# Decay exponents from a bf16 product per four heads, a first block on weight differences, and a new order of the products, in a Mamba-2 scan with a maxout feed-forward

## The chip, the cores and the metric

The kernel runs on one core of a Trainium2 chip. Its engines are TensorE (PE: matrix products into PSUM; PEld is its weight load), VectorE (DVE), ScalarE (ACT), GpSimd (POOL) and SyncE (SP), which here issues the DMAs. Each engine works through its own instructions in program order and waits on semaphores for the others. The metric is the device time of one execution in microseconds (us), as the median of several runs.

## What is computed

Four batches of 768 tokens with eight heads go through a state-space scan, and the 3072 x 256 result goes through a maxout feed-forward with three 256 x 768 matrices and an output matrix:

```
log_a = np.log(np.clip(a, 1e-06, 1.0))
cum = np.cumsum(la, axis=-1)
L = np.exp(cum[:, :, :, None] - cum[:, :, None, :])
L = L * causal
CB = np.einsum('bhin,bhjn->bhij', Cc, Bc)
M = CB * L
y_intra = np.einsum('bhij,bhjd->bhid', M, xc)
y_inter = np.einsum('bhin,bhnd->bhid', Cc, state) * decay_to_i[:, :, :, None]
...
h = np.maximum(np.maximum(x @ w1, x @ w2), x @ w3)
return (h @ w_out).astype(np.float32)
```

The weights arrive as 64-bit floats, and the kernel turns them into 32-bit ones itself.

## The kernel before, in words

The sequence is cut into six blocks of 128 tokens (c = 0 to 5), each for all four batches (512 columns) and all eight heads. **Block 0** is computed in plain fp32: its scan, then the three up products for six feature groups of 128 (18 groups, n = 0 to 17, in the loop at L962, products L589 and L597; an fp32 product stands in the trace as two rows), then its output products (`first_down`, L780, products L792) which run inside block 1. **Blocks 1 to 5** use the three weight matrices as a base and two differences: max(x w1, x w2, x w3) = x w2 + max(x (w1-w2), x (w3-w2), 0). Every operand is split into a near part H, a far part L and a crossed part S (`split_steps` L612 for weights, `scan_y` L560 for the scan's output, `late` L710 for h), so that three fast products (fp32r) replace a slow one. A block has twelve units u, six feature groups f by two differences i. In each unit `early` (L704) makes the near and far products (`near_far` L687, products L692) into one of two up banks of PSUM and scales their sum (`raise_sum` L697, on ACT in even units and on DVE in odd ones); `late` (L710) adds the crossed products (L717) of the unit before and takes the maximum: ACT copies m (L722) for i = 0, DVE makes h (L726) and H (L730) for i = 1, POOL makes L (L731). `down_next` (L822, products L811) makes the output of the block before.

**Weights.** SP fetches twelve pieces of 512 KB (`fetch` L163). `decode` (L215) starts the conversion of one piece: ACT L191 and L200, DVE L192 and L195, POOL L201; `sign` (L221) ends it with DVE L206. In the loop over the 18 groups a sign and a decode stand at every second group. `behind` (L671) issues the steps that form and split the differences (POOL L637 and L626, ACT L625 and L622, DVE L628).

**Decays.** The scan needs L = exp(cum_i - cum_j) for 128 x 128 positions of each batch and head. SP writes the running sums to DRAM (L887) and reads them back spread over all partitions: `decay_load` L387 fills L (1 MB for two batches), `last_load` L394 fills E (eight DMAs a block). POOL masks L (`decay_masks` L400, L402), ACT takes the exponential head by head with the bias -cum_j (`decay_part` L406, L409: 128 columns an instruction, 32 a block). DVE multiplies the scores s (L501) with L (`scan_weight` L507, L509); `scan_old` and `scan_own` (L515, L530) make y, and the next block's products need y. The scan of block n = c + 1 is worked in among block c's units. s, y, A, trB, trC, w2T and fold share four att banks of PSUM.

The order is written out by hand: the strings FIRST, STEADY and LAST (L1036 to L1067) give the words of each unit, which `act` (L1069) turns into calls: Z is `early`, p `late`, d `down_next`, q `first_down`, x and z parts of the exponentials, m and n masks, b steps of `behind`, t, c, e, s0, s2, A, y the steps of the scan, a number so many waiting steps of `later`.

## Time and profile before

| | |
|---|---|
| median of 3 runs | 293.43 us (292.38 to 297.33) |
| profiled execution | 294.27 us, span 292.6 us, mean granted clock 0.975 |
| busy in the span | PE 257.2 us (88%), DVE 177.7 (61%), ACT 144.6 (49%), POOL 117.9 (40%) |
| chain that ended last | PE 54%, DVE 19%, DMA 6%, SP's queue 5%, ACT 5%, POOL 4% |
| DMA | 28.13 MB in 105018 packets, of which L from cums takes 10 DMAs of 1 MB and E 40 of 32 KB |

The span is the time from the first to the last instruction of one profiled execution; the profiled execution took 1.7 us more than its span. Busy shares are means over stages: an opening of block 0, five blocks of twelve units, and a short end. Which wait ends last in a stage is read from the waits and the timeline of that stage.

### The profile page before, as it was taken

How to read it: one execution, taken by the hardware profiler on the slowest of the kernel's cores; microseconds unless marked ns; L12 is line 12 of the kernel's file. 1: busy time of each engine (PE TensorE's matmuls, PEld its weight loads, DVE VectorE, ACT ScalarE, POOL GpSimd, SP SyncE). 2: the span in 40 equal slices, each digit the busy share in tenths (PEclk: the TensorE clock that was granted, in tenths of full speed). 3: DMA queues.
4: the chain of work that ended last, by engine and by line, in shares of the span. 5: the costliest groups of instructions: out<-in, count | busy, mean ns of one | idle time of the engine just before them, and what ended most of it. 6: DMA issues, size and time to landing. Idle time of an engine off the chain costs nothing.

```text
span 292.6 us, 5239 instructions
## 1 busy us (share of the span) xinstructions
PE 257.2 (88%) x2030; PEld 197.6 (68%) x2030; DVE 177.7 (61%) x283; ACT 144.6 (49%) x336; POOL 117.9 (40%) x105
## 2 busy tenths in 40 slices
PE   6899992897986899879899798999898999999994
PEld 4665340446855578758678586787686787979993
DVE  2586757699666454285673865766645838445452
ACT  2775745694598423785315475416573332222211
POOL 5173668318975525354151541534211113112321
PEclk9999999799999879979999999999999999999999
DMA  7979998986999110488500779101000002002002
GB/s 83 177 280 273 144 258 148 211 188 168 209 182 128 40 36 1 100 220 83 69 2 2 210 187 130 14 3 64 10 0 0 2 2 73 0 2 72 0 3 72
DMA packets 105018, 28.13 MB, mean 96 GB/s; under 512 B 75297, under 2 KB 101921, under 8 KB 104993
## 3 DMA queue, kind: packets, MB, share of 16 engines
q1 hardware_dynamic: 104688, 27.66, 46.6%
q8 instruction: 16, 0.26, 0.4%
q10 hardware_dynamic: 304, 0.13, 0.2%
q14 instruction: 10, 0.07, 0.1%
HBM read 24.54 MB, written 3.24 MB: 95 GB/s over the span
## 4 chain that ended last, share of the span: by engine, by line
PE 54%; DVE 19%; DMA 6%; SPq 5%; ACT 5%; POOL 4%; issue 4%; POOLq 1%; DVEq 0%; ACTq 0%
PE up L692 15%; PE o L811 14%; PE up L717 7%; PE s L501 4%; SPq L173 3%; PE o L792 3%; DVE L L509 2%; DVE yS L577 2%; PE up L597 2%; DMA rb<-in_moe_w_dram 2%; DMA raw_C<-in_C_dram 2%; SPq L139 2%; DVE h L726 2%; PE y L537 2%; DVE yL L569 2%
## 5 line engine op out<-in xcount | busy, mean ns | idle before, releaser
L731 POOL TENSOR_TENSOR hL<-h,hH 128x512 fp32r<-128x512 f32 x30 | 39.0, 1299 | 121.4 <-DVE hH L730 106.7
L726 DVE SCALAR_TENSOR_TENSOR h<-up,m 128x512 f32<-128x512 f32 x30 | 20.7, 691 | 49.8 <-PE up L717 34.7
L409 ACT ACTIVATE L<-L,ncums 128x128 f32<-128x128 f32 x160 | 50.1, 394 | 0.0
L692 PE MATMUL up<-yH,wH 128*128 128x512 f32 x120 | 42.6, 437 | 4.2 <-ACT m L722 3.0
L717 PE MATMUL up<-yS,wS 128*128 128x512 f32 x120 | 38.7, 404 | 3.0 <-DVE up L701 2.9
L692 PE MATMUL up<-yL,wL 128*128 128x512 f32 x120 | 39.2, 407 | 1.8 <-DVE yL L569 1.7
L699 ACT ACTIVATE up<-up 128x512 f32<-128x512 f32 x30 | 17.5, 582 | 45.6 <-PE up L692 45.6
L722 ACT COPY m<-up 128x512 f32<-128x512 f32 x30 | 17.5, 584 | 40.6 <-PE up L717 40.3
L597 PE MATMUL up<-yT,w 128*128 128x512 f32 x64 | 30.6, 622 | 2.5 <-DVE w L206 2.4
L701 DVE TENSOR_SCALAR up<-up 128x512 f32<-128x512 f32 x30 | 20.9, 695 | 18.4 <-PE up L692 18.4
L509 DVE TENSOR_TENSOR L<-s,L 128x512 f32<-128x512 f32 x46 | 29.2, 681 | 4.0 <-PE s L501 4.0
L717 PEld LDWEIGHTS up<-yS,wS 128*128 128x128 f32 x120 | 22.6, 192 | 9.9 <-DVE up L701 4.4
L692 PEld LDWEIGHTS up<-yL,wL 128*128 128x128 f32 x120 | 23.3, 194 | 8.6 <-DVE yL L569 3.2
L201 POOL TENSOR_TENSOR w_u<-w_u,w_r 128x512 uint32<-128x512 uint32 x12 | 15.3, 1271 | 30.7 <-DVE w_u L195 18.9
L402 POOL TENSOR_SCALAR_AFFINE_SELECT L<-L 128x1024 f32<-128x1024 f32 x20 | 25.9, 1319 | 0.0
L501 PE MATMUL s<-CT,BT 32*128 32x256 f32 x192 | 17.2, 415 | 9.0 <-ACT CT L443 6.0
L597 PEld LDWEIGHTS up<-yT,w 128*128 128x128 f32 x64 | 12.1, 198 | 18.5 <-issue 13.6
L692 PEld LDWEIGHTS up<-yH,wH 128*128 128x128 f32 x120 | 19.4, 194 | 7.6 <-ACT m L722 3.6
L577 DVE SCALAR_TENSOR_TENSOR hS<-hL,hH 128x512 fp32r<-128x512 f32 x30 | 23.4, 782 | 1.5 <-POOL hL L731 1.5
L811 PE MATMUL o<-wH,hH 128*128 128x256 f32 x120 | 21.1, 294 | 1.1 <-DVE ob L839 1.1
L811 PEld LDWEIGHTS o<-wH,hH 128*128 128x128 f32 x120 | 18.5, 194 | 4.8 <-DVE ob L839 1.7
L811 PE MATMUL o<-wS,hS 128*128 128x256 f32 x120 | 19.2, 289 | 2.0 <-DVE o L701 1.1
(117 smaller groups left out, 413.2 us busy)
## 6 DMA issues: line engine op xcount, KB each, us to landing
L<-cums SPq DMA_DIRECT2D x10, 1024.0 KB, 9.8
rb<-in_moe_w_dram SPq DMA_DIRECT2D x9, 512.0 KB, 6.7
raw_x<-in_x_dram SPq DMA_DIRECT2D x6, 512.0 KB, 7.6
out_dram<-ob SPq DMA_DIRECT2D x12, 256.0 KB, 2.1
raw_B<-in_B_dram SPq DMA_DIRECT2D x6, 256.0 KB, 4.7
raw_C<-in_C_dram SPq DMA_DIRECT2D x6, 256.0 KB, 6.9
rb<-in_moe_w_out_dram SPq DMA_DIRECT2D x3, 512.0 KB, 5.1
E<-cums SPq DMA_DIRECT2D x40, 32.0 KB, 4.3
```

What stands on the lines that cost most here:

```text
L402: nc.gpsimd.affine_select(out=Ls[c][:, b], in_=Ls[c][:, b], pattern=[[0, NH], [1, P]], compare_op=ALU.is_ge, fill=MASKED, base=0, channel_ ...
L409: nc.scalar.activation(L[:, b, h], L[:, b, h], AF.Exp, bias=ncum[c][:, b * NH + h:b * NH + h + 1], scale=1.0)
L501: nc.tensor.matmul(out=s[:, i].rearrange("j g i -> j (g i)"), lhsT=st["BT"][rows, b], rhs=st["CT"][rows, b].rearrange("p g i -> p (g i)"), ...
L509: nc.vector.tensor_tensor(out=M, in0=s, in1=M, op=ALU.mult)
L577: nc.vector.scalar_tensor_tensor(out=out, in0=L, scalar=-RAISE, in1=H, op0=ALU.mult, op1=ALU.add)
L597: nc.tensor.matmul(out=bank, lhsT=w_of(i, k, f), rhs=yT[0][:, k], start=(k == 0), stop=(k == KD - 1))
L692: nc.tensor.matmul(out=bank, lhsT=up_parts[q, i][z][:, k, g * P:(g + 1) * P], rhs=y_parts[c][z][:, k], start=(z == 0 and k == 0), stop=(z ...
L701: nc.vector.tensor_scalar(out=bank, in0=bank, scalar1=1.0 + 1.0 / RAISE, scalar2=None, op0=ALU.mult)
L717: nc.tensor.matmul(out=up, lhsT=up_parts[q, i][2][:, k, g * P:(g + 1) * P], rhs=y_parts[c][2][:, k], start=False, stop=(k == KD - 1), skip ...
L726: nc.vector.scalar_tensor_tensor(out=h, in0=up, scalar=0.0, in1=held["m"], op0=ALU.max, op1=ALU.max)
L731: nc.gpsimd.tensor_tensor(out=L, in0=h, in1=plain(H), op=ALU.subtract)
L811: nc.tensor.matmul(out=o[b // 2][:, b % 2], lhsT=left[:, b * P:(b + 1) * P], rhs=right, start=(first and b % 2 == 0), stop=True, skip_grou ...
```

## The change

**Decays.** The running sums are split into three bf16 parts whose sum is the fp32 value (`sums_first`, `sums_store`) and written to DRAM once. `left` (128 rows: for each of the 32 batch-heads three part rows and one of ones) and `right` (the head's indicator times -1, and for each batch the part rows of the block, loaded by `rows_right`) make cum_i - cum_j for four heads as one bf16 product of 32 rows by 512 columns (`decay_pair`: two batches, two products in two row groups of PE, two att banks). `decay_exp` takes the exponential of 512 columns at once from PSUM, and after the second one POOL sets the masked half to zero. E comes from four bf16 products with `esel` in place of eight DMAs. The loads of L and E, and the transposed sums, are gone.

**First block.** Only the first two feature groups use the three weight matrices directly (n = 0 to 5). The other four use the differences, with max(.., 0) in place of the third product (n = 6 to 13), so 14 groups stand in place of 18; the base's share comes back by `first_base`, products of y with the folded base matrix, in block 1. `first_down` is cut into twelve pieces by weight pair and batch, nine of them in the opening. A sign and a decode stand at each of the first ten groups. Eight weight pieces (`NFETCH`) are fetched right behind the first block's inputs, four of them into a tile of the L pool, and the order of the pieces is changed.

**Products.** `early` is split into `near` and `far`, with `late` of the unit before between them; `raise_sum` of up is on ACT in every unit, and H of h moves from DVE to ACT (`halve`). Each weight split has a tile `rest` of its own, and the order of paired splits is changed.

The diff, cut to its core:

```diff
-        weight_jobs.append(
+        weight_jobs.insert(
+            (5, 10, 11)[o // 2],
             (wo_raw, part.rearrange("(o p) m -> p o m", p=P), moe_w_out.dtype))
...
+    early = att.tile([P, 4, 2, WCOL, 2], U32, tag="L", name="early")
+    ahead += [early[:, n] for n in range(4)]
     load(0, "B")
     load(0, "C")
...
-    fetch()
-    fetch()
-
+    for _ in range(NFETCH):
+        fetch()
...
+    by_tile = ident.rearrange("p (t h q) -> p t h q", t=REP, q=4)
+    ind = const.tile([P, NH], FP32, name="ind")
+    nc.vector.tensor_reduce(
+        out=ind, in_=by_tile[:, :, :, 0:3].rearrange("p t h q -> p h q t"),
+        op=ALU.add, axis=AX.XY)
+    own = const.tile([P, REP, NH], FP32, name="own")
+    nc.vector.tensor_reduce(out=own, in_=by_tile[:, :, :, 0:3], op=ALU.add, axis=AX.X)
...
+    def rows_minus(n):
+        nc.scalar.mul(right[n], ind.unsqueeze(2).to_broadcast([P, NH, P]), -1.0)
...
-    cums = dram.tile([BH, NC, P], FP32, name="cums")
-
-    def decay_load(c, pairs=(0, 2)):
-        L = decays(c) if 0 in pairs else Ls[c]
-        for b in pairs:
+    RT = P // REP
+    sums = dram.tile([3, BH, NC, P], BF16, name="sums")
...
-                out=L[:, b:b + 2].rearrange("j b h i -> j (b h) i"),
-                in_=cums[b * NH:(b + 2) * NH, c, :].partition_broadcast(P))
-
-    def last_load(c):
-        E = blocks[c]["E"] = half([HN, NB, P], "E")
-        rows = cums[:, c].rearrange("(b h) s -> h b s", h=NH)
-        for h in range(NH):
-            nc.sync.dma_start(out=E[h * N:(h + 1) * N], in_=rows[h].partition_broadcast(N))
...
-    def decay_masks(c, bs):
-        for b in bs:
-            nc.gpsimd.affine_select(
-                out=Ls[c][:, b], in_=Ls[c][:, b], pattern=[[0, NH], [1, P]],
-                compare_op=ALU.is_ge, fill=MASKED, base=0, channel_multiplier=-1)
-
-    def decay_part(c, b, g):
-        L = Ls[c]
-        for h in range(g * HALF, (g + 1) * HALF):
-            nc.scalar.activation(
-                L[:, b, h], L[:, b, h], AF.Exp,
-                bias=ncum[c][:, b * NH + h:b * NH + h + 1], scale=1.0)
...
+
+    hl = half([R, 3, 2, P], "hl", BF16)
+    rest = half([R, 2, P], "sums_rest")
+
+    def sums_first():
+        nc.scalar.copy(out=hl[:, 0], in_=a_sb)
+        nc.vector.tensor_tensor(out=rest, in0=a_sb, in1=hl[:, 0], op=ALU.subtract)
+
+    def sums_store():
+        nc.scalar.copy(out=hl[:, 1], in_=rest)
+        nc.vector.tensor_tensor(out=hl[:, 2], in0=rest, in1=hl[:, 1], op=ALU.subtract)
+        for p in range(3):
             nc.sync.dma_start(
-                out=L[:, b:b + 2].rearrange("j b h i -> j (b h) i"),
-                in_=cums[b * NH:(b + 2) * NH, c, :].partition_broadcast(P))
-
-    def last_load(c):
-        E = blocks[c]["E"] = half([HN, NB, P], "E")
-        rows = cums[:, c].rearrange("(b h) s -> h b s", h=NH)
-        for h in range(NH):
-            nc.sync.dma_start(out=E[h * N:(h + 1) * N], in_=rows[h].partition_broadcast(N))
-
-    def decay_masks(c, bs):
-        for b in bs:
-            nc.gpsimd.affine_select(
-                out=Ls[c][:, b], in_=Ls[c][:, b], pattern=[[0, NH], [1, P]],
-                compare_op=ALU.is_ge, fill=MASKED, base=0, channel_multiplier=-1)
-
-    def decay_part(c, b, g):
-        L = Ls[c]
-        for h in range(g * HALF, (g + 1) * HALF):
-            nc.scalar.activation(
-                L[:, b, h], L[:, b, h], AF.Exp,
-                bias=ncum[c][:, b * NH + h:b * NH + h + 1], scale=1.0)
-
+                out=sums[p].rearrange("k c s -> (k c) s").rearrange("(w r) s -> r w s", w=2),
+                in_=hl[:, p])
+
+    def rows_right(c):
+        for p in range(3):
+            nc.sync.dma_start(
+                out=right[c % 2][4 * p + 3::RT],
+                in_=sums[p, :, c].rearrange("(b h) i -> b h i", h=NH))
+
+    def rows_left():
+        for p in range(3):
+            nc.sync.dma_start(
+                out=left[p::4].rearrange("r c i -> r (c i)"),
+                in_=sums[p, :, 1:].rearrange("r c i -> r (c i)"))
+
+    def decay_pair(c, b0, g):
+        L = decays(c) if (b0, g) == (0, 0) else Ls[c]
+        heads = slice(g * HALF, (g + 1) * HALF)
+        es = [att_bank([P, HALF, P], "e") for _ in range(2)]
+        for i, e in enumerate(es):
+            rows = slice((b0 + i) * RT, (b0 + i + 1) * RT)
+            nc.tensor.matmul(
+                out=e.rearrange("p k i -> p (k i)"), lhsT=left[rows, c - 1],
+                rhs=right[c % 2][rows, heads].rearrange("p k i -> p (k i)"),
+                start=True, stop=True, tile_position=((b0 + i) * RT, 0), skip_group_check=True)
+        exps.extend((L, b0, heads, i, e) for i, e in enumerate(es))
+
+    exps = []
+
+    def decay_exp():
+        L, b0, heads, i, e = exps.pop(0)
+        nc.scalar.activation(L[:, b0 + i, heads], e, AF.Exp)
+        if i == 0:
+            return
+        part = L[:, b0:b0 + 2, heads]
+        nc.gpsimd.affine_select(
+            out=part, in_=part, pattern=[[0, 2], [0, HALF], [1, P]],
+            compare_op=ALU.is_ge, fill=0.0, base=0, channel_multiplier=-1)
...
     def scan_e(c):
-        E = blocks[c]["E"]
-        nc.scalar.activation(E, E, AF.Exp)
+        e = att_bank([HN, NB, P], "E")
+        for b in range(NB):
+            nc.tensor.matmul(
+                out=e[:, b], lhsT=esel[:, b * NH:(b + 1) * NH].rearrange("p h n -> p (h n)"),
+                rhs=left[:, c - 1], start=(b == 0), stop=True, skip_group_check=True)
+        E = blocks[c]["E"] = half([HN, NB, P], "E")
+        nc.scalar.activation(E, e, AF.Exp)
...
     def paired(one, two):
-        order = (0, 0, 1, 1, 2, 3, 2, 4, 3, 4)
-        which = (0, 1, 0, 1, 0, 0, 1, 0, 1, 1)
+        order = (0, 0, 1, 2, 1, 3, 4, 2, 3, 4)
+        which = (0, 1, 0, 0, 1, 0, 0, 1, 1, 1)
...
-    def early(c, u):
-        up = up_bank([P, BLK], "up")
-        near_far(up, c, u)
-        raise_sum(up, nc.vector if u % 2 else nc.scalar)
+    def near(c, u):
+        held["up"] = up_bank([P, BLK], "up")
+        near_far(held["up"], c, u, 0)
+
+    def far(c, u):
+        up = held["up"]
+        near_far(up, c, u, 1)
+        raise_sum(up, nc.scalar)
         opened.append((c, u, up))
...
+        held["h"] = c, f, h
+
+    def halve():
+
+        if "h" not in held:
+            return
+        c, f, h = held.pop("h")
         H, L = (half([P, BLK], "h" + n, F32R) for n in "HL")
         h_parts[c][f] = [H, L]
-        nc.vector.tensor_scalar(out=H, in0=h, scalar1=NEAR, scalar2=None, op0=ALU.mult)
+        nc.scalar.mul(H, h, NEAR)
...
-            based["steps"] = [(k, f) for k in range(KD) for f in range(NF)]
+            based["steps"] = [(k, f) for half_ in (range(2, NF), range(2))
+                              for k in range(KD) for f in half_]
...
+            if (k, f) == (KD - 1, NF - 1):
+                based["first"] = to = half([P, KD, DM], "fold0")
+                nc.scalar.copy(out=to, in_=based["sum"])
...
+    def first_base():
+        u, i = bases.pop(0)
+        o = held["o0", u]
         b = 2 * u + i
-        n = NF // 2
-        for f in range(half_ * n, (half_ + 1) * n):
+        for k in range(KD):
             nc.tensor.matmul(
-                out=o[:, i], lhsT=h0[f][:, b * P:(b + 1) * P], rhs=wo_raw[f // 2][:, f % 2],
-                start=(f == 0), stop=(f == NF - 1), skip_group_check=True)
-        if j % 4 == 3:
+                out=o[:, i], lhsT=yT[0][:, k, b * P:(b + 1) * P], rhs=based["first"][:, k],
+                start=False, stop=True, skip_group_check=True)
...
-    nc.sync.dma_start(
-        out=cums.rearrange("k c s -> (k c) s").rearrange("(w r) s -> r w s", w=2), in_=a_sb)
-    fetch()
-    decay_load(1, (0,))
-    fetch()
-    decay_load(1, (2,))
-    fetch()
-    load(1, "B")
...
+    sums_first()
...
+    sums_store()
...
+
+        if n < 6:
+            i, g = divmod(n, 2)
+            f, kind = g, ("copy", "max", "max")[i]
+            of = lambda k: w_of(i, k, f)
+        else:
+            q, i, g = 1 + (n - 6) // 4, (n - 6) // 2 % 2, n % 2
+            f, kind = 2 * q + g, ("copy", "max0")[i]
+            of = lambda k: differences[q, i][:, k, g * P:(g + 1) * P]
...
+        if kind == "copy":
+            h0[f] = half([P, BLK], "h0")
+            nc.scalar.copy(out=h0[f], in_=p)
+        elif kind == "max":
+            nc.vector.tensor_tensor(out=h0[f], in0=h0[f], in1=p, op=ALU.max)
         else:
-            p = pair[g]
...
-        if n >= 6:
-            behind(1)
-        if n == 11:
-            transposed(1)
-            scan_c(1)
-        if n == 12:
-            scan_e(1)
...
+    OPENING = (
+        "n0 sign B1 rows decode fj "
+        "n1 sign decode C1 fetch x1 "
+        "n2 sign decode bt fetch "
+        "n3 sign bu1:1 decode fetch "
+        "n4 sign decode minus "
+        "n5 sign bu1:1 decode "
+        "n6 q t X0 E E sign decode "
+        "n7 q c sign bu2:1 X1 E decode E e 1 "
+        "n8 q X2 E E sign bu2:1 decode "
+        "n9 q s0 2 sign 2 decode "
+        "n10 bu0:2 X3 E sign bd bu0:2 E "
+        "n11 q s2 2 bu0:2 "
+        "n12 q 2 load2 bu0:2 "
+        "n13 q A y q bu0:2 9 "
+    )
     FIRST = [
-        "Z sign tc b2 load m01",
-        "Z p sign g c e b2 q",
-        "Z p 1 x2 g m23 b2 q q",
-        "Z p x2 q b2",
-        "Z p s0 x1 b2 q",
-        "Z p 4 x2 g b3 q",
-        "Z p x1 s2 b3 n01 q",
-        "Z p 4 A b2 q",
-        "Z p 1 G6 b4",
-        "Z p G6 z2 b4 d d",
-        "Z p y b4 d 2 d",
-        "Z p 2 n23 z3 d d",
+        "Z X0 E bu1:2 E load q",
+        "Z X1 E bu1:2 g q E",
+        "Z t bu1:2 g q",
+        "Z c e 1 bu1:2 q",
+        "Z s0 1 bu2:2 1",
+        "Z 1 g 1 bu2:2 bo:2 G4",
+        "Z X2 E bu2:2 bo:2 E G4",
+        "Z X3 E bu2:2 bo:2 G4 E",
+        "Z s2 1 bo:2 r 1",
+        "Z 1 bo:4 1 A r r",
+        "Z y 1 r d d 2 d",
+        "Z W0 E d 2 E d W1 d E E",
     ]
     STEADY = [
-        "Z p x1 d d load",
-        "Z p t d d",
-        "Z p c e d d x1",
-        "Z p 1 s0 d d 2",
-        "Z p d 2 d x1 n01",
-        "Z p d s2 d 2",
-        "Z p d 2 d A",
-        "Z p 1 d y d z1",
-        "Z p 2 d d 2",
-        "Z p z1 n23 d d",
-        "Z p d d z1",
-        "Z p d d z2",
+        "Z t d d load",
...
+        "Z s2 d 1 d 1",
...
+        "Z W1 d E d E",
...
                 if word == "Z":
-                    early(c, u)
+                    near(c, u)
+                    late()
+                    far(c, u)
+                    halve()
                 else:
```

Three places show how the order on the engines moves. The first is POOL (GpSimd), from the first product of block 0's feed-forward to the middle of the opening; `w_u` is the sum of a decode, `d` a weight difference, AFFINE_SELECT on `L` the mask, `Bd` the scaled B. Before:

```order
L201 TENSOR_TENSOR w_u<-w_u,w_r 128x512 x3
L402 AFFINE_SELECT L<-L 128x1024 x2
L201 TENSOR_TENSOR w_u<-w_u,w_r 128x512 x2
L637 TENSOR_TENSOR d<-w 128x512 x2
L201 TENSOR_TENSOR w_u<-w_u,w_r 128x512
L402 AFFINE_SELECT L<-L 128x1024 x2
L201 TENSOR_TENSOR w_u<-w_u,w_r 128x512
L626 TENSOR_TENSOR d<-d,wH 128x512
L459 TENSOR_TENSOR Bd<-raw_B,from_js 128x512
L201 TENSOR_TENSOR w_u<-w_u,w_r 128x512
```

and now, from the third decode on to the last mask before the scores of batches 2 and 3 are weighted:

```order
L208 TENSOR_TENSOR w_u<-w_u,w_r 128x512 x2
L695 TENSOR_TENSOR d<-w 128x512
L208 TENSOR_TENSOR w_u<-w_u,w_r 128x512
L464 AFFINE_SELECT L<-L 128x2x512
L208 TENSOR_TENSOR w_u<-w_u,w_r 128x512
L695 TENSOR_TENSOR d<-w 128x512
L208 TENSOR_TENSOR w_u<-w_u,w_r 128x512
L464 AFFINE_SELECT L<-L 128x2x512 x2
L695 TENSOR_TENSOR d<-w 128x512
L208 TENSOR_TENSOR w_u<-w_u,w_r 128x512 x2
L695 TENSOR_TENSOR d<-w 128x512 x2
L518 TENSOR_TENSOR Bd<-raw_B,from_js 128x512
```

Each mask and each difference now stands between two decodes, and the fourth mask of block 1 stands behind the last decode, two differences, Bd and one split (the next row but one, not shown).

The second place is PE in a unit of block 2, where B and C of the next block are transposed (`trB`, `trC`); wH and wL are the weights' near and far parts, wS their crossed part. Before, and then now:

```order
L811 MATMUL o<-wL,hL 128x256 x4
L692 MATMUL up<-yH,wH 128x512 x2
L692 MATMUL up<-yL,wL 128x512 x2
L717 MATMUL up<-yS,wS 128x512 x2
L428 MATMUL trB<-ident,raw_B 128x128 x4
```

```order
L886 MATMUL o<-wL,hL 128x256 x4
L741 MATMUL up<-yH,wH 128x512 x2
L770 MATMUL up<-yS,wS 128x512 x2
L741 MATMUL up<-yL,wL 128x512 x2
L482 MATMUL trB<-ident,raw_B 128x128 x4
```

The crossed products of the unit before now come ahead of the unit's own far products.

The third place is ACT over some units around the start of a block; the ACTIVATE on `up` is `raise_sum`, COPY to `m` and `hH` belong to `late` and `halve`, and the ACTIVATE on `L` is an exponential. Before, and then now:

```order
L699 ACTIVATE up<-up 128x512
L409 ACTIVATE L<-L,ncums 128x128 x4
L722 COPY m<-up 128x512
L409 ACTIVATE L<-L,ncums 128x128 x8
L699 ACTIVATE up<-up 128x512
L409 ACTIVATE L<-L,ncums 128x128 x4
```

```order
L748 ACTIVATE up<-up 128x512
L460 ACTIVATE L<-e 128x512 x4
L748 ACTIVATE up<-up 128x512
L790 ACTIVATE hH<-h 128x512
L478 COPY BT<-trB 128x512
L775 COPY m<-up 128x512
L748 ACTIVATE up<-up 128x512
```

The exponentials are fewer and wider, and every unit has a `raise_sum` on ACT, every second one an H.

## Rows read from the trace of the kernel before

**Rows 1.** Window, length, busy us of PE, PEld, DVE, ACT, POOL, clock, DMA, GB/s.

```profile
18.95:68.79 49.84, 42.68 (x287) 22.14 (x287) 36.48 (x57) 31.77 (x73) 26.34 (x22) 0.97 0.89 194
68.79:126.69 57.90, 47.91 (x345) 37.46 (x344) 31.99 (x47) 33.26 (x81) 34.35 (x29) 0.94 0.60 116
126.69:169.81 43.12, 39.63 (x336) 31.98 (x337) 30.09 (x47) 21.81 (x57) 16.53 (x14) 0.96 0.50 96
169.81:210.69 40.88, 37.67 (x339) 30.97 (x338) 26.30 (x41) 20.55 (x53) 15.18 (x13) 1.00 0.37 63
210.69:249.38 38.69, 36.93 (x307) 30.51 (x305) 23.40 (x40) 16.93 (x40) 7.76 (x6) 1.00 0.04 15
```

**Rows 2.** PE's waits in block 1: us in total, times, longest.

```profile
PE w2T_tp L752 <- DVE L L509: 2.4, 1, 2.4
PE A L469 <- DVE L L509: 1.7, 1, 1.7
PE up L692 <- DVE yL L569: 1.4, 1, 1.4
PE up L692 <- ACT m L722: 1.3, 1, 1.3
PE up L692 <- DVE h L726: 1.2, 1, 1.2
```

**Rows 3.** Timeline of the decodes: start, length, engine, line, idle before.

```profile
22.09 0.69 DVE L206 SCALAR_TENSOR_TENSOR w<-rb,w_u 128x512 uint32<-128x512 uint32 x1 [1.44 <-POOL w_u L201]
26.59 0.69 DVE L206 SCALAR_TENSOR_TENSOR w<-rb,w_u 128x512 uint32<-128x512 uint32 x1 [0.27 <-POOL w_u L201]
...
34.22 0.69 DVE L206 SCALAR_TENSOR_TENSOR w<-rb,w_u 128x512 uint32<-128x512 uint32 x1 [0.85 <-POOL w_u L201]
35.00 0.43 DVE L192 TENSOR_SCALAR w_u<-w_u 128x512 f32<-128x512 f32 x1
...
36.03 1.26 POOL L201 TENSOR_TENSOR w_u<-w_u,w_r 128x512 uint32<-128x512 uint32 x1 [1.84 <-ACT h L983]
37.26 2.93 POOL L637 TENSOR_TENSOR d<-w 128x512 f32<-128x512 f32 x2
...
37.59 1.48 DVE L206 SCALAR_TENSOR_TENSOR w<-rb,w_u 128x512 uint32<-128x512 uint32 x1
```

**Rows 4.** Lines L206 and L192: ns min/median/max, first and last start.

```profile
L206 DVE SCALAR_TENSOR_TENSOR w<-rb,w_u x12: 674/692/1733, 17.2 to 74.8; 128x512 uint32<-128x512 uint32 x12
L192 DVE TENSOR_SCALAR w_u<-w_u x12: 398/427/1308, 14.0 to 67.6; 128x512 f32<-128x512 f32 x12
```

**Rows 5.** Groups by line: count | busy us, mean ns | idle before.

```profile
L402 POOL TENSOR_SCALAR_AFFINE_SELECT L<-L 128x1024 f32<-128x1024 f32 x20 | 25.9, 1319 | 0.0
L509 DVE TENSOR_TENSOR L<-s,L 128x512 f32<-128x512 f32 x46 | 29.2, 681 | 4.0 <-PE s L501 4.0
L701 DVE TENSOR_SCALAR up<-up 128x512 f32<-128x512 f32 x30 | 20.9, 695 | 18.4 <-PE up L692 18.4
L409 ACT ACTIVATE L<-L,ncums 128x128 f32<-128x128 f32 x160 | 50.1, 394 | 0.0
L370 ACT ACTIVATE L<-spread 128x512 f32<-128x512 f32 x4 | 2.2, 599 | 3.7 <-PE spread L350 3.7
```

**Rows 6.** Timeline of PE: products alone and two waits.

```profile
2.50 1.87 PE L322 MATMUL spread<-mask,ident 128*128 128x512 bf16 x4 [2.50 <-POOL mask L259]
...
27.43 11.24 PE L597 MATMUL up<-yT,w 128*128 128x512 f32 x24
...
140.40 1.10 PE L501 MATMUL s<-CT,BT 32*128 32x256 f32 x10 [1.01 <-DVE Cd L454]
...
147.57 1.15 PE L501 MATMUL s<-CT,BT 32*128 32x256 f32 x16
155.33 1.95 PE L537 MATMUL y<-L,raw_x 128*32 128x128 f32 x64
...
165.78 0.73 PE L717 MATMUL up<-yS,wS 128*128 128x512 f32 x2 [1.41 <-DVE up L701]
```

More of the change, by code (lines that the diff above doesn't have):

```diff
@@ L969 @@
             first_own((2, 3))
[L970 to L971 removed]
+            group(held["pair"][1], 0, 1, (0,))
+            for p, ff in zip(held["pair"], range(2)):
                 group(p, 0, ff, (1,))
[L973 removed]
+        if n < 2:
+            p = held["pair"][n]
+        else:
             p = ffn_bank([P, BLK], "up")
[L975 to L979 removed]
@@ L1083, in act @@
         elif word == "decode":
-            decode()
+            if fetched:
+                decode()
+        elif word == "fetch":
+            fetch()
+        elif word == "fj":
+            held["fj"] = from_last(R, a_sb, "fj")
+        elif word == "bt":
+            from_js = by_token(R, held["fj"], "from_js", 1.0, att_bank)
+            for m in range(1, NC):
+                from_j[m] = from_js[:, :, m]
+        elif word == "bd":
+            scan_bd(n)
         elif word[0] == "b":
-            behind(int(word[1:]))
-        elif word == "tc":
-            scan_tc(n, att_bank)
+            name, m = word[1:].split(":")
+            behind(name, int(m))
         elif word == "t":
             transposed(n)
+            if c and n < NC - 1:
+                scan_bd(n)
         elif word == "c":
```

229 lines of the change are left out of this document (107 added, 122 removed).

## The prediction, made before the changed kernel ran

> **What bounds the kernel now.** I read the windows by stage first [rows 1]: the opening (the first feed-forward product of block 0 at 18.95 us to the first near product of block 1 at 68.79) takes 49.8 us, block 1 57.9, blocks 2, 3 and 4 43.1, 40.9 and 38.7; block 5 and the end take what is left of the span, 292.6 - 249.4 = 43.2. In blocks 2 to 4 PE is busy for 39.6, 37.7 and 36.9 us of these: there PE is the bound, and at most 3.5 us a block can be won without taking work from it. In the opening PE is idle for 7.2 us and in block 1 for 10.0, and the granted clock is below 1 in both (0.97 and 0.94). So the question is what the change does to 107.7 us of opening and block 1.
>
> Second, the waits of PE in block 1 [rows 2]: 6.7 of 8.0 us named end with DVE (2.4 + 1.7 + 1.4 + 1.2), 1.3 with ACT. DMA is no releaser there, though its share is 0.60: what the removed loads weigh in bytes says nothing by itself.
>
> Third, the decodes in the opening's timeline [rows 3]. A sign (DVE, 0.69) is followed by two DVE operations of 0.43, the sum on POOL (1.26), and the next sign. From the sign at 34.22 to the next at 37.59 are 3.4 us; the four operations alone make 0.69 + 0.43 + 0.43 + 1.26 = 2.8, with the steps between engines about 3.1. Before, a new decode comes with every second group of products, and a group takes 4 rows of 11.24/24 = 0.47, that is 1.9 us [rows 6], so two groups (3.8) cover one round. Afterwards a decode comes with every group.
>
> **The opening, step by step.** PE loses 4 groups (7.5 us) and gains nine `first_down` pieces of 4 rows of 256 columns, at half of 0.47 each (9 x 0.94 = 8.4 us), and four pairs of decay products. PE's own work is then 42.7 - 7.5 + 8.4 + 1.7 (the pairs and E, priced below) = 45.3, and alone it would end the stage at 64.2. What decides is the round of the decodes. The sign at group 0 keeps its place, 22.1, and the next follows at 26.6 as before [rows 3], since ACT's step waits for group 0's copy. Up to the sign at group 10 nine more rounds follow. Three have nothing between: 3 x 3.1 = 9.3. Two have a weight difference on POOL behind the sign, at 1.4 (two took 2.93 [rows 3]), half of it beside DVE's two steps: 3.8 each, 7.6. One has a mask (1.32 [rows 5]): 4.0; one a difference: 3.9; one has two masks and a difference: 5.6; one has two products with L on DVE (0.68 each [rows 5]) ahead: 4.2. The sum is 26.6 + 34.6 = 61.2 for that sign, and POOL's last sum ends a moment earlier. Behind it POOL still has two differences, Bd, a split and the fourth mask, five operations of about 1.3, to 67.6; DVE weights the last scores with it (2 x 0.68), to 68.9; the products of y then finish in about 2 us (1.95 for the own ones [rows 6]), and ACT's copy of y takes 0.6. Block 1 starts at 71.5, **2.7 us later** than now. Fetching earlier takes away DMA as a releaser of the decodes, but the rounds take the time.
>
> The rest of the opening's edits I cost at nothing: the two reductions, `rows_minus` and the split of the sums lie on DVE and ACT in idle time ahead of the first exponentials or in place of the removed transposes of the sums (0.3 us if that cover is gone). The small loads of `left` and `right` stand on SP behind nine weight pieces and the first inputs, 5.7 MB, which at the stage's 194 GB/s [rows 1] are through at about 29 us; the first pair stands behind group 6, whose difference isn't there before 34. Behind these loads on SP wait C and x of block 1, used at groups 6 and 13: 5 us of cover for C, the thinnest of these.
>
> **Block 1.** PE loses the 48 rows of `first_down` and gets 12 of them back and 16 of `first_base`: 20 rows x 0.23 = 4.7 less. It gains six pairs of decay products, four small products for E and a transpose. A pair is an operation that no row here shows. Upper bound: the four bf16 products of 512 columns at the start took 1.87, so 0.47 each and 0.94 a pair [rows 6]. Lower bound: both run side by side in their row groups at 0.23, as the sixteen rows of s do, which take 1.15 us where a row of 256 columns at 0.23 would make 3.7 one after the other [rows 6]. I take 0.35, nearer to s, whose tiles have the same 32 rows: 2.1 for six, 3.0 with E (0.3) and trB (0.6). Net 1.7 us less: 46.2. Its clock was 0.94 over the stage; with shorter gaps I count 0.97, 1.4 us less: 44.8. DVE loses six `raise_sum` of 0.70 [rows 5], six H and two signs, about 8.8 of its 32.0 us. Its 6.7 us of waits I take to fall to a third, 2.2. ACT gives 13 parts of four exponentials, 52 at 0.39, for 12 at 0.60 [rows 5], and gains six `raise_sum`, six H and one copy at 0.6: -20.3 + 7.2 + 7.8, so 5 us less at most (less than that, since exponentials that follow each other overlap); I halve its 1.3 us of waits to 0.7. With the 2.0 us of small gaps, idle is 4.9. Block 1 takes 49.7, **8.2 us less**.
>
> **Blocks 2 to 4.** Removed: PE's wait of 1.4 for `raise_sum` on DVE in two of them, of which the one in block 2 stands in the rows [rows 6]; part of the wait of 1.0 for Cd before s (three times, 0.3 each; trC still holds a bank until E's exponential is done); 1.5 of low clock in block 2. Added: four pairs and E in two blocks (1.7 each), two pairs and E in block 4 (1.0). -2.8 - 0.9 - 1.5 + 4.4 = **-0.8**. The new place of the crossed products shortens the cover of `raise_sum`: far products, other products (0.95), near products (0.46), then late. `raise_sum` takes 0.6 on ACT, so 1.4 us cover it, unless ACT is behind by more than 0.6. Block 5 is unchanged but for H on ACT at its very end: +0.2.
>
> **The sum.** 2.7 - 8.2 - 0.8 + 0.2 = -6.1 on the profiled execution's span of 292.6: 286.5, with the 1.7 around it 288.2. The median of the runs is 0.8 under the profiled execution: 287.3, and I say **287.0**.
>
> **The rivals.** *Opening at PE's pace.* If the rounds run at 3.1 throughout, because POOL's masks and differences find gaps (it is busy for 26.3 of 49.8 us now [rows 1]), block 1 starts at 64.2 instead of 71.5, and with PE steadily fed the idle time of block 1 falls to 2.5: 287.0 - 7.3 - 2.4 = **277.3**. Against it: POOL gains some 7 us of work in the stage, and its order is fixed.
>
> *Waits that stay.* The sums of up all move to ACT, with H and the exponentials between; if ACT is late for the crossed products as DVE was, block 1 keeps its 10 us of idle (+5.1), and if the pairs run one after the other, sixteen of them cost 0.12 more each (+1.9): **294**. For it: ACT is in order, and a split's L on it waits for POOL. Against it: its total in block 1 does not grow. This is also the case in which the change does not do what it says: the loads of L were hidden, and taking them away frees nothing.
>
> *DVE and POOL block each other.* A sign took 1.48 while POOL worked on two differences, 0.69 otherwise [rows 3], and at most 1.73; the first DVE step took 1.31 at most against 0.43 [rows 4]. If every one of the ten rounds meets a mask or a difference in this way, each is 1.04 + 0.88 = 1.9 longer, 19 in all, less the 5.6 that the five rounds with POOL's work in them have above 3.1 already: 13.4 later, **300.4**, slower than before. It decides from 1.8 us a round on (12.3 us above my sum, to 299.3). For it: masks and differences now stand between the decodes. Against it: the median of the twelve signs is still 0.69 [rows 4], so at least half of them met nothing, and the price needs every round at its worst. The Trainium skill, page "SBUF — State Buffer", section "SBUF: two separate sides", has a rule for this: a DVE instruction with two SBUF inputs or in a two-port mode and a POOL instruction take a shared pair of ports by an exclusive lock, and the loser waits for the whole of the other. By that rule each meeting would cost up to a whole POOL operation, and the trace agrees in the one sign shown.
>
> **How the numbers follow.** My forecast (281 to 292) gets 0.45, the opening at PE's pace 0.25, waits that stay 0.22, blocking 0.08. About 2% is also what a measurement of this kernel can tell from no change. Faster by over 2% means under 287.6: all of the second case and a little over half of the first, 0.51. Slower means over 299.3: the blocking case and a tail of the waits, 0.12. Within 2%: 0.37. The range reaches from just under the middle of the second case, 276, to 297, above the waits that stay; half of the second case and the blocking case are left out, about 0.2.
>
> **What would show it.** Right: the first near product of block 1 at 70 to 73 us, signs 3 to 4 us apart and nearly 6 at the two masks, block 1 near 50 us with DVE's releases of PE mostly gone, blocks 2 to 4 within 1 us of now, a pair of decay products at 0.25 to 0.5. Wrong: block 1 starting before 66 or after 76; PE waiting for ACT's `raise_sum` in every unit; PE waiting for the loads of `right`; a block 3 more than 2 us away from 40.9. An error in the opening's rounds would be the first thing to look for, since one us a round moves the time by ten.

## The result and the profile after

The changed kernel takes 278.55 us (median of 4 runs, 277.98 to 278.77); the kernel before takes 292.9 beside it (293.43 and 292.38). The ratio is 0.9507, with a 95% interval of 0.9469 to 0.9545: faster by about 5%. Some executions of most of these kernels are about 2% longer at a lower granted clock (in four of the five profiles of that kind, those of e3, e5, e7, e9 and e11, PE waits 1.8 to 2.4 us for x of block 0), so the times leave them out, and of these five profiles only waits, the blocks behind the opening, or one such opening beside another is read. In three later sets of runs the kernel before had medians of 291.5 to 292.0, while the changed kernel, run again (e5), had 277.99. So the gain is nearer to 13.5 us, and the one profiled execution of the kernel before (292.6 of span, 1.7 around it) lies some 2.5 us above its other runs. Stage differences of 2 us against that one execution are therefore not to be trusted.

The windows by stage of the changed kernel: the opening, blocks 1 to 4, block 5 with the end (columns as in [rows 1]).

```profile
19.13:74.17 55.04, 47.98 (x311) 26.16 (x311) 38.02 (x59) 27.06 (x50) 33.05 (x28) 0.91 0.88 135
74.17:120.66 46.49, 45.42 (x348) 33.94 (x347) 28.34 (x37) 33.74 (x64) 23.82 (x20) 1.00 0.09 18
120.66:158.96 38.30, 38.30 (x351) 30.78 (x349) 19.14 (x28) 21.52 (x42) 15.71 (x14) 1.00 0.38 46
158.96:197.19 38.23, 38.23 (x350) 30.77 (x349) 19.56 (x29) 21.29 (x41) 15.17 (x13) 1.00 0.29 34
197.19:233.66 36.47, 36.47 (x314) 30.20 (x313) 17.60 (x28) 19.79 (x37) 11.50 (x9) 1.00 0.04 15
233.66:276.90 43.24, 37.96 (x244) 34.15 (x242) 12.71 (x19) 16.06 (x29) 9.04 (x7) 0.98 0.07 25
```

Against [rows 1] the opening became 5.2 us longer (forecast +2.7), block 1 11.4 shorter (forecast -8.2), blocks 2 to 4 together 9.7 shorter (forecast -0.8), block 5 the same. In blocks 2 to 4 PE's busy time equals the stage: it is never idle for a step that these rows show, and the clock is 1.00 from block 1 to block 4. (A busy row can hide a short wait: in block 4 the 16 rows of the first scores take 1.71 us, those of the second 1.15.)

PE's waits over the whole execution of the changed kernel (releaser: us in total, times, longest us), to be set against [rows 2]; three more are of 0.5 at most:

```profile
PE up L1040 <- POOL d L695: 3.6, 1, 3.6
PE e L450 <- DVE L L568: 3.2, 1, 3.2
PE spread L346 <- POOL mask L267: 2.5, 1, 2.5
PE s L560 <- ACT CT L497: 1.4, 1, 1.4
PE o L886 <- ACT o L748: 0.7, 1, 0.7
PE up L648 <- ACT yT L614: 0.7, 1, 0.7
...
```

The five waits of [rows 2] are gone, and so are those for Cd and up of [rows 6]. The two largest stand in the opening, and both are new. The timeline of the changed kernel's opening: two signs and two DVE steps (answering [rows 3]), then PE around its two waits.

```profile
43.35 1.56 DVE L213 SCALAR_TENSOR_TENSOR w<-rb,w_u 128x512 uint32<-128x512 uint32 x1 [1.45 <-POOL w_u L208]
...
52.55 1.31 DVE L199 TENSOR_SCALAR w_u<-w_u 128x512 f32<-128x512 f32 x1
53.90 1.37 DVE L202 TENSOR_SCALAR w_u<-w_u 128x512 uint32<-128x512 uint32 x1
...
61.09 1.73 DVE L213 SCALAR_TENSOR_TENSOR w<-rb,w_u 128x512 uint32<-128x512 uint32 x1 [1.44 <-POOL w_u L208]
```

```profile
34.85 2.52 PE L1040 MATMUL up<-yT,d 128*128 128x512 f32 x4 [3.64 <-POOL d L695]
...
51.33 1.98 PE L1040 MATMUL up<-yT,d 128*128 128x512 f32 x4
56.51 1.18 PE L450 MATMUL e<-right,left 32*128 32x512 bf16 x2 [3.19 <-DVE L L568]
57.62 3.78 PE L1040 MATMUL up<-yT,d 128*128 128x512 f32 x4
61.19 1.91 PE L854 MATMUL o<-w,h 128*128 128x256 f32 x4
```

The sign at group 10 starts at 61.09, where the walk through the rounds gave 61.2. The rest of the stage is PE's own: behind the wait that ends at 56.5 it has no further one, and up to 63.0 its granted clock is 0.51, the lower of its two levels: four rows take 3.78 instead of 1.98, and the four of 256 columns behind them 1.91 where they otherwise take 1.03.

The groups by line that answer [rows 4] and [rows 5] (a line of decode steps with min/median/max, then count | busy us, mean ns | idle before), of the changed kernel:

```profile
L199 DVE TENSOR_SCALAR w_u<-w_u x12: 398/419/1309, 14.2 to 58.8; 128x512 f32<-128x512 f32 x12
```

```profile
L748 ACT ACTIVATE up<-up 128x512 f32<-128x512 f32 x60 | 35.4, 590 | 39.7 <-PE up L741 39.6
...
L460 ACT ACTIVATE L<-e 128x512 f32<-128x512 f32 x40 | 22.8, 603 | 3.6 <-PE e L450 3.6
```

160 exponentials of 50.1 us became 40 of 22.8; ACT took on 30 sums and 30 near halves in their place.

### The profile page after: what moved, and what is told of

Its sections match the earlier page's. It is cut to its first block, busy times and chain, and to the rows that moved or that the text cites. A ratio compares the mean times of both kernels' runs of the same rounds, so it can differ in the third digit from the quotient of the medians.

```text
span 276.9 us, 5133 instructions
## 1 busy us (share of the span) xinstructions
PE 258.9 (93%) x2088; PEld 196.6 (71%) x2088; DVE 146.0 (53%) x222; ACT 151.7 (55%) x281; POOL 117.7 (42%) x107
## 4 chain that ended last, share of the span: by engine, by line
PE 78%; ACT 7%; DVE 7%; POOL 3%; issue 3%; POOLq 1%; ACTq 0%
PE o L886 20%; PE up L741 19%; PE up L770 9%; PE s L560 5%; PE y L596 3%; PE o L854 3%; PE up L1040 3%; POOL w_u L208 2%; PE e L450 2%; PE fold L826 2%; PE y L583 2%; DVE w L213 2%; PE spread L362 1%; PE o L867 1%; ACT L L460 1%
## 5 line engine op out<-in xcount | busy, mean ns | idle before, releaser
L748 ACT ACTIVATE up<-up 128x512 f32<-128x512 f32 x60 | 35.4, 590 | 39.7 <-PE up L741 39.6
L636 DVE SCALAR_TENSOR_TENSOR hS<-hL,hH 128x512 fp32r<-128x512 f32 x30 | 27.2, 907 | 35.9 <-POOL hL L791 35.9
L741 PE MATMUL up<-yH,wH 128*128 128x512 f32 x120 | 40.2, 416 | 0.1
L741 PE MATMUL up<-yL,wL 128*128 128x512 f32 x120 | 37.5, 392 | 0.1
L464 POOL TENSOR_SCALAR_AFFINE_SELECT L<-L 128x1024 f32<-128x1024 f32 x20 | 24.0, 1202 | 11.4 <-ACT L L460 11.3
L460 ACT ACTIVATE L<-e 128x512 f32<-128x512 f32 x40 | 22.8, 603 | 3.6 <-PE e L450 3.6
L1040 PE MATMUL up<-yT,d 128*128 128x512 f32 x32 | 18.1, 692 | 3.6 <-POOL d L695 3.6
L790 ACT ACTIVATE hH<-h 128x512 fp32r<-128x512 f32 x30 | 18.7, 625 | 4.3 <-DVE h L779 4.3
L560 PE MATMUL s<-CT,BT 32*128 32x256 f32 x192 | 18.5, 411 | 1.8 <-ACT CT L497 1.4
L886 PE MATMUL o<-wL,hL 128*128 128x256 f32 x120 | 19.6, 284 | 0.0
```

What stands on the lines that cost most here:

```text
L460: nc.scalar.activation(L[:, b0 + i, heads], e, AF.Exp)
L464: nc.gpsimd.affine_select(out=part, in_=part, pattern=[[0, 2], [0, HALF], [1, P]], compare_op=ALU.is_ge, fill=0.0, base=0, channel_multipl ...
L560: nc.tensor.matmul(out=s[:, i].rearrange("j g i -> j (g i)"), lhsT=st["BT"][rows, b], rhs=st["CT"][rows, b].rearrange("p g i -> p (g i)"), ...
L636: nc.vector.scalar_tensor_tensor(out=out, in0=L, scalar=-RAISE, in1=H, op0=ALU.mult, op1=ALU.add)
L741: nc.tensor.matmul(out=bank, lhsT=up_parts[q, i][z][:, k, g * P:(g + 1) * P], rhs=y_parts[c][z][:, k], start=(z == 0 and k == 0), stop=(z ...
L748: nc.scalar.mul(bank, bank, 1.0 + 1.0 / RAISE)
```

## The experiments

Two questions were put: which part of the change emptied blocks 2 to 4 of waits, and what holds the opening. No run takes block 1's gain apart.

### Which part gave the blocks their time

**Both edits of the products undone (e10).** Decays by pairs, the first block on differences and the new plan of a unit's words (STEADY and the like) stay; the order of the products and the engines of the sums are those of before.

```
 near(c, u)
-late()
 far(c, u)
+if len(opened) > 1: late()
...
-raise_sum(up, nc.scalar)
+raise_sum(up, nc.vector if u % 2 else nc.scalar)
-nc.scalar.mul(H, h, NEAR)
+nc.vector.tensor_scalar(out=H, in0=h, scalar1=NEAR, ...)
```

> The changed kernel with both edits of the products undone: near, far, crossed of the unit before, odd sums and the near halves of h on DVE, as in the kernel before. What is left of the change are the decays by pairs and the first block on differences. Theory A (the decays alone freed DVE and ACT, and that took the waits of the blocks away): 280 to 283, blocks 2 to 4 within 3 us of the changed kernel in sum. Theory B (order and engines were needed together): 286 or more, blocks 2 to 4 at least 6 us longer in sum, PE waiting for DVE's up and h.

Measured: 279.89 us (median), ratio 0.9604 [0.9563, 0.9644]. Its windows of blocks 1 to 4, and PE's waits in blocks 2 to 4:

```profile
74.12:120.68 46.56, 45.50 (x348) 34.04 (x347) 33.71 (x48) 28.34 (x53) 25.15 (x20) 1.00 0.09 18
120.68:159.61 38.93, 38.64 (x351) 30.93 (x350) 25.19 (x40) 15.82 (x30) 15.11 (x14) 1.00 0.40 47
159.61:198.45 38.84, 38.55 (x350) 30.89 (x349) 25.58 (x41) 15.55 (x29) 14.44 (x13) 1.00 0.24 32
198.45:235.46 37.01, 36.69 (x315) 30.27 (x313) 24.34 (x40) 13.74 (x25) 10.99 (x9) 1.00 0.05 15
```

```profile
PE up L741 <- DVE h L779: 0.9, 3, 0.3
```

Theory A held, with the time 0.1 under its span. Blocks 2 to 4 take 114.8 us, against 122.7 of [rows 1] and 113.0 of the whole change; PE's idle time in them is 0.9 us, against 8.5 before. Block 1 is already at 46.6. So the two edits of the products are not what emptied the blocks: the decays by pairs did it, or the new plan that came with them.

The load of an engine doesn't tell which. In e10 ACT is lighter than before (45.1 us in blocks 2 to 4, for 59.3 in [rows 1]) and DVE is not in blocks 3 and 4 (25.6 and 24.3 for 26.3 and 23.4); in the whole change it is DVE that is lighter (56.3 for 79.8) and ACT heavier (62.6), and PE hardly waits in either. What PE waited for in these blocks of the kernel before says more:

```profile
PE s L501 <- DVE Cd L454: 3.0, 3, 1.0
PE up L717 <- DVE up L701: 2.9, 2, 1.4
...
PE o L811 <- DVE o L701: 1.1, 3, 0.4
PE o L811 <- DVE ob L839: 1.1, 3, 0.4
PE up L692 <- DVE yL L569: 0.3, 1, 0.3
```

These are 8.4 of the 8.5 us of idle time, and every one ends with DVE, none with ACT. In the four larger groups DVE had something else ahead in its order. Block 2 before (E's exponential on ACT had ended at 138.15), and block 2 of e10 (where it ended at 127.78):

```profile
138.32 0.70 DVE L701 TENSOR_SCALAR up<-up 128x512 f32<-128x512 f32 x1 [0.82 <-PE up L692]
...
139.57 0.68 DVE L454 TENSOR_TENSOR Cd<-trC,E 128x512 f32<-128x512 f32 x1
...
162.31 2.80 DVE L577 SCALAR_TENSOR_TENSOR yS<-yL,yH 128x512 fp32r<-128x512 f32 x2
165.04 0.69 DVE L701 TENSOR_SCALAR up<-up 128x512 f32<-128x512 f32 x1
```

```profile
127.82 0.69 DVE L513 TENSOR_TENSOR Cd<-trC,E 128x512 f32<-128x512 f32 x1 [1.27 <-ACT E L506]
...
152.05 0.69 DVE L750 TENSOR_SCALAR up<-up 128x512 f32<-128x512 f32 x1
...
154.69 1.28 DVE L636 SCALAR_TENSOR_TENSOR yS<-yL,yH 128x512 fp32r<-128x512 f32 x2
```

Before, Cd stood on DVE behind a unit's sum and the crossed part hS, and PE's scores came right behind it; in the new plan Cd is written a unit ahead of the scores, and DVE starts it as soon as E is there. Before, the sum of unit 9 stood behind yL, ob and yS, two of which took 2.80 us while POOL masked L (161.99 to 164.57); now it stands ahead of them, and the two yS take 1.28. The sums of o and ob have moved ahead in the same way. So at these places, as the traces show them, the waits went with the new order on DVE and the new place of POOL's masks; whether the new plan would have done the same beside the loaded decays is not shown, since no run has the one without the other.

**The order alone undone (e9).** The sums stay on ACT.

```
 near(c, u)
-late()
 far(c, u)
+if len(opened) > 1: late()
```

> The changed kernel with the order of the crossed products undone: near, far, then the crossed products of the unit before, as in the kernel before, with the lag of one unit kept; all else as changed (sums and halves on ACT, decays by pairs, first block on differences). Theory A (the blocks gained because ACT and DVE have room, so any order that keeps the lag finds its sums ready): 278 to 281, PE without a wait over 0.3 in blocks 2 to 4. Theory B (the order itself took the waits away): 283 or more, with waits of PE at the crossed products for up of 3 us or more in sum.

Measured: 278.88 us, ratio 0.9564 [0.9514, 0.9615]. The windows of its blocks 2 to 4:

```profile
125.93:164.29 38.36, 38.36 (x351) 30.88 (x349) 19.19 (x28) 21.95 (x42) 15.73 (x14) 1.00 0.38 46
164.29:202.62 38.33, 38.33 (x350) 30.85 (x349) 19.56 (x29) 21.72 (x41) 15.18 (x13) 1.00 0.31 34
202.62:239.32 36.70, 36.70 (x314) 30.39 (x313) 17.62 (x28) 20.20 (x37) 11.50 (x9) 1.00 0.04 15
```

113.4 us for 113.0: the order is worth nothing that can be measured here. Theory A.

**Odd sums and the near halves back on DVE (e1)**, the last four lines of the diff of e10 alone, with the new order.

> The changed kernel with the sums of up in odd units and H of h back on DVE; the rest stays. Theory: blocks 2 to 4 lost their PE idle time (3.5, 3.2 and 1.8 us before) because DVE was relieved of six sums (0.70) and six H (0.44) a block; put back, most of it returns: 1 to 2.5 us a block in blocks 1 to 4, so 284 +- 2 against 278.6, with PE waiting for DVE up again. Rival: the relief came from the exponentials and loads of L that are gone; then this run stays within 1 us of 278.6.

Measured: 280.66 us, ratio 0.962 [0.9501, 0.9739], between the two expectations. PE waits in it for DVE's sums, 1.3 us in four waits. The same edit parts e10 from e9 (1.0 us), and in the profiles blocks 2 to 4 take 1.3 us more in e1 than in the changed kernel and 1.4 more in e10 than in e9: moving this work to ACT is worth 1 to 2 us.

**The two edits of the products alone, in the kernel before (e12).**

```
-near_far(up, c, u)
-raise_sum(up, nc.vector if u % 2 else nc.scalar)
+near_far(up, c, u, 0)
+late()
+near_far(up, c, u, 1)
+raise_sum(up, nc.scalar)
...
-nc.vector.tensor_scalar(out=H, in0=h, scalar1=NEAR, ...)
+nc.scalar.mul(H, h, NEAR)
```

> The kernel before with the two edits of the products alone: crossed products between near and far, all sums and the near halves of h on ACT; decays and first block as before. Theory A (the decays are what gave the blocks their time): 293 to 299 against 293 to 296 of before, since ACT has 60 sums more than it had beside 160 exponentials. Theory B (the product edits gave it): 287 or less, waits of PE for up and Cd gone in blocks 2 to 4.

Measured: 290.44 us, ratio 0.9957 [0.9931, 0.9984], 1.2 us under the 291.6 of the kernel before: a small gain where theory A has none, and far from theory B. PE's waits in its blocks 2 to 4:

```profile
PE up L719 <- ACT up L699: 2.0, 4, 0.6
PE s L501 <- DVE Cd L454: 1.9, 3, 0.6
...
```

Without the rest of the change, the sums that left DVE make PE wait for ACT, and Cd still comes late. PE's idle time in these blocks is 6.4 us; the kernel before had 8.5.

**The order alone, in the kernel before (e7)**: the first part of the diff of e12, with the odd sums left on DVE.

> The kernel before with the one edit that the crossed products of the unit before stand between near and far products; sums still alternate between ACT and DVE, decays are still loaded. Theory: with sums alternating the order is worth at most 1 to 2 us either way: ratio 0.99 to 1.01. Rival: the order is worth most of what blocks 2 to 4 gained (9.7 us): ratio 0.97 or less.

Measured: 297.2 us against 291.5, ratio 1.0208 [1.0115, 1.0301]: slower, which neither expectation had. PE's largest wait and that for Cd in it:

```profile
PE up L719 <- DVE up L701: 8.7, 5, 2.5
...
PE s L501 <- DVE Cd L454: 4.0, 3, 1.3
```

The new order leaves fewer products between a sum and the crossed products that need it. With DVE as loaded as before, the sum comes late; [rows 6] has one such wait of 1.41, here there are five of up to 2.5.

**Two runs with the lag of a unit lost (e2, e6).** They were meant as "the order undone", but calling `late()` behind `far` without the condition of e9 makes it take the unit just appended: each crossed product waits for its own sum.

> The changed kernel with the products of a unit in the old order (near, far, then the crossed ones of the unit before). Theory: the order alone moves little, since a sum on ACT has 1.4 us of cover either way: 278.6 +- 1. Rival: the new order is what took PE's waits away, because it frees an up bank half a microsecond earlier: then 3 us or more longer, with PE waiting at the near products for m or h.

> The changed kernel with both edits of the products undone: near, far, then the crossed ones, odd sums and H of h on DVE; decays, opening and first block stay new. Each alone gave: sums on DVE about +2 to 3 us, old order with all sums on ACT +67 us, where PE waited 49.6 us for the sums. Theory: that 67 us came of the sum of unit u standing on ACT ahead of the copy of unit u-1, which the alternation of ACT and DVE avoids; so with both undone the time is 280 to 285, and the decays alone carry most of the gain in blocks 1 to 4. Rival: the order itself is needed whatever engine sums: 290 or more.

Measured: 345.88 us, ratio 1.1866 [1.1718, 1.2014], and 342.3 us. The wait of PE in e2:

```profile
PE up L770 <- ACT up L748: 49.6, 59, 2.7
```

They say nothing on the order of before. They price the lag: a sum with no cover costs PE 0.84 us of wait a unit, 49.6 in all, and the time grew by 67 us.

**Each decay product issued twice (e4).**

```
+for _ in range(2):
   nc.tensor.matmul(out=e..., lhsT=left[rows, c - 1], ...)
```

> The changed kernel with each decay product issued twice (the same result). The 22 pairs start 0.31 to 0.32 us ahead of the next product. Theory: PE is without idle time in blocks 1 to 4, so the 18 pairs there cost their full time once more and the four in the opening little: +5 to +6 us, 284. Rival: the two products of a pair run one behind the other (0.47): +8; or PE has slack there: under +2.

Measured: 281.93 us, ratio 0.97 [0.9547, 0.9854]: 3.4 us over the changed kernel, between the theory and "under +2". There are 20 pairs, 16 of them from block 1 on, not the 22 and 18 of the expectation. E's four products and a pair in block 3 of the changed kernel, and the doubled pair at the same place, each with the product behind it (start, length):

```profile
164.52 0.40 PE L502 MATMUL E<-left,esel 128*128 128x128 bf16 x4
164.72 0.71 PE L741 MATMUL up<-yH,wH 128*128 128x512 f32 x2
...
172.76 0.39 PE L450 MATMUL e<-right,left 32*128 32x512 bf16 x2
173.08 0.74 PE L886 MATMUL o<-wH,hH 128*128 128x256 f32 x4
```

```profile
174.67 0.61 PE L451 MATMUL e<-right,left 32*128 32x512 bf16 x4
175.20 0.74 PE L887 MATMUL o<-wH,hH 128*128 128x256 f32 x4
```

From a pair to the next product are 0.32 us, from a doubled one 0.53. A further pair, two products of 512 columns, thus costs 0.21, as much as E's four bf16 products of 128 columns together (0.20): the two products of a pair run side by side. The 0.47 of [rows 6], from which the prediction has its upper bound, is more than twice as much for one such product; those four are PE's first in the kernel, and no row shows why they are slower. The sixteen pairs from block 1 on at 0.21 make 3.4 us; in the profile blocks 1 to 4 take 163.2 us for 159.5, 3.7 more, and PE's idle time there is 1.1 in both. So in the blocks PE has no slack, and what it is given shows in full.

### What holds the opening

**Four groups of the first block issued twice (e8)**, groups 6 to 9: 16 rows more, 7.5 us of PE.

```
-for k in range(KD):
+for rep in range(2 if 6 <= n <= 9 else 1):
+  for k in range(KD):
     nc.tensor.matmul(out=p, lhsT=of(k), rhs=yT[0][:, k], ...)
```

> The changed kernel with four of block 0's groups (n = 6 to 9) issued twice into the same bank: 16 rows, 7.5 us of PE at 0.47. Theory of the prediction: the opening is set by the rounds of the decodes, so most of it hides: under +2 us. Rival: from group 6 on PE is the bound as well (the trace shows it without a gap from 34.85 to 53.3): +5 to +8, with the wait of 3.2 before the fourth pair taking up part of it.

Measured: 283.3 us, ratio 0.9755 [0.9667, 0.9844]; block 1 starts at 77.85 where the changed kernel has 74.17. The opening's window, to be set against the first one above:

```profile
19.16:77.85 58.69, 52.96 (x327) 28.81 (x327) 36.61 (x59) 27.23 (x50) 32.78 (x28) 0.94 0.82 126
```

The wait of 3.2 for the fourth pair is gone, another of 2.1 stands behind it:

```profile
PE s L560 <- ACT L L460: 2.1, 1, 2.1
```

The result lies between the two expectations: +4.8 us by the medians, +3.7 by the start of block 1. If the rounds alone set the end, the added products would have filled waits and cost nothing. Of the 7.5 us added, PE's idle time took up only 1.3 (5.7 us for 7.1); about half showed, and the rest, 2.5, fits the higher clock (0.94 for 0.91). From group 6 on PE is a bound beside the rounds.

**The decode ahead of the sign in each slot (e3)**, so that DVE doesn't stand idle for POOL's sum:

```
-"n0 sign B1 rows decode fj "
+"n0 decode sign B1 rows fj "
-"n1 sign decode C1 fetch x1 "
+"n1 decode sign C1 fetch x1 "
...
```

> The changed kernel with each group's decode written ahead of its sign, so that two decodes are under way and a sign doesn't wait for the POOL sum that the same round started. Theory: the opening is set by the round of sign, two DVE steps and POOL sum (signs at 22.7 to 61.1, 3.8 us a round); with two under way a round costs DVE's 1.6 plus 0.7 and POOL's 1.3 to 2.7: about 2.8, and block 1 starts 4 to 8 us before 74.2; time 271 to 275. Rival: PE's own work, POOL's order or the clock bind the opening as much: at most 1.5 us shorter.

Measured: 275.59 us, ratio 0.9441 [0.9315, 0.9566], some 3 us under the changed kernel; the intervals overlap. That is just above the theory's span. In its profile the opening takes 55.3 us, where it takes 57.0 in e5 and 57.9 in e9, which have the opening of the changed kernel: a gain is likely, and not shown.

**The opening eased further (e11)**: e3, with the fourth pair behind group 11 and two differences earlier.

```
-"n9 q s0 2 decode sign 2 "
+"n9 q s0 2 sign 2 bu0:2 decode "
-"n10 bu0:2 X3 E sign bd bu0:2 E "
+"n10 sign bd bu0:2 "
-"n11 q s2 2 bu0:2 "
+"n11 X3 E E bu0:2 q s2 2 "
```

> The changed kernel with the opening written in another order: each decode ahead of the sign of its slot, the fourth pair of decay products behind group 11 instead of group 10, and the first two differences of block 0's weights at group 9. Theory (rounds and the wait for the fourth pair's banks hold the opening, 3.6 and 3.2 us of waits with a low clock behind each): 272 to 276, block 1 starts at 68 to 71. Rival (PE's own work from group 6 on sets the end): 276 to 278.6, block 1 starts not before 72.

Measured: 278.55 and 275.76 us, ratio 0.9505 [0.9409, 0.9601]: one lies in the rival's span, the other just inside the theory's, so the times don't decide. The profile speaks against the theory: the opening takes 57.2 us, where it takes 57.0 in e5. PE's waits up to block 1:

```profile
PE up L1040 <- POOL d L695: 2.9, 1, 2.9
...
PE up L1040 <- DVE w L213: 2.0, 1, 2.0
```

The wait of 3.2 was taken away, and one of 2.0 for a sign and smaller ones came in its place. No version that is surely better than the changed kernel came of this; e3 is the best by its median.

## Why the prediction was right in sign and wrong in its parts

The time of 278.55 lies inside the range of 276 to 297, 8.5 us under the forecast of 287.0 and close to the 277.3 of the rival "opening at PE's pace". That is luck: the rival's road was not taken (it has block 1 start at 64.2, and it starts at 74.2), and a stage that came out worse than forecast was covered by two that came out better. One of the signs that the prediction gave for being wrong is there: block 3 takes 38.2 us, 2.7 away from 40.9.

**The opening: +5.2 for +2.7.** The walk through the rounds was right, round by round: the last sign at 61.09 for 61.2, POOL's last mask ends at 67.3 for 67.6, DVE's last weights at 68.6 for 68.9. Two things failed behind it. The step "PE's own work ... alone would end the stage at 64.2" treated PE and the rounds as two bounds of which the later counts. PE's work comes in order, so the waits for the difference (3.6) and for the fourth pair's banks (3.2) pushed all behind them back; with 48.0 us busy and 7.1 idle PE itself ends the stage, at 74.2, without a wait from 56.5 on. And its clock over the stage was 0.91, not the 0.97 in which the 45.3 us were reckoned: behind the two waits it was at the lower level for some 3.4 and 6.4 us (0.64 over 4.8 us and 0.51 over 6.5). The wait for the fourth pair was not in the sum at all: att banks that scores hold until DVE has weighted them.

**Block 1: -11.4 for -8.2.** The idle time fell, as forecast, but to 1.1 us where I left 4.9, and not for the reason given: DVE's load fell by 3.7 us, not 8.8, and ACT's rose by 0.5; in e10's block 1 DVE is busy for 33.7 us, more than before, and PE is idle for 1.1 there too. PE's busy time of 45.4, for the 44.8 of the sum, agrees by luck. The 46.2 of the sum before its clock term are reckoned at 0.94, and at the measured clock of 1.00 they would have been 43.4; in e12's profile, where block 1 of the old kind runs at 1.00 in 55.1 us, PE is busy for 45.6, so its work did not fall. Which part of the change emptied this block no run shows.

**Blocks 2 to 4: -9.7 for -0.8.** This is the mis-sized term, and it alone is larger than the whole forecast gain. I removed the waits that I could name (2.8 + 0.9 + 1.5) and charged the pairs and E in full (4.4). Of idle time 8.5 us went, where the sum removes 3.7. The 2.8 for DVE's sums was right (2.9). The wait for Cd was taken to fall by a third, 0.9, and fell by all of 3.0, since its new place in the plan gives it a unit of cover; the waits for the sums of o and for ob (2.2) were left out without a reason. PE's busy time fell by 1.2, where the clock term and the charge together raise it by 2.9: a pair cost 0.32 for 0.35 and E 0.20 for 0.3, and busy time in block 3 rose by 0.6 us, not 1.7; where the rest of the charge went is open. What stays open too is how much of this the new plan would give without the cheaper decays. Some 2.5 us of the 9.7 and the 11.4 may belong to the one execution of before, which had a clock of 0.94 in block 1, where e12 has 1.00.

**The new place of the crossed products.** I costed it at nothing as long as ACT isn't late, and that is what e9 shows. The condition mattered: beside a loaded DVE the same order loses 5.7 us (e7).

**Waits that stay.** The rival's two prices fell with the profile: PE waits for ACT's sums nowhere in blocks 1 to 4, and the pairs run side by side.

**DVE and POOL block each other.** Signs of 1.56, 1.56 and 1.73 and DVE steps of 1.3 to 1.4 stand beside POOL's work, at the sizes forecast, but the median of the decode step is 0.42 (its longest 1.31, as in [rows 4]) and the rounds ended where the walk had them. The price was paid elsewhere: ahead of the weights that PE's wait of 3.2 us ends with, two DVE steps took 1.31 and 1.37 us instead of 0.42 and 0.43 beside POOL's mask and difference. The Trainium skill, page "SBUF — State Buffer", section "SBUF: two separate sides", has DVE and POOL lock a shared pair of ports; the trace agrees with it in size where they meet, and they met in about half of the eleven rounds.

## What to carry to other kernels

Where the bound engine is idle for a few per cent in a steady stage, add up the idle time and look, for every wait, at what stands ahead of the releaser in its own order. Here nearly all of the waits in blocks 2 to 4 ended with a step of DVE that stood behind other steps of DVE, and they went when those steps changed places; the total load of ACT or of DVE didn't tell it. Two bounds of one stage don't simply give the later of the two when the bound engine runs in order, since a gap early in its queue is paid in full at its end. And an order that shortens the cover of a step is free only as long as the engine that does the step is on time; try it with the load of that engine as it is.
